# One attention-plus-MLP kernel: a pair's scores in two chained four-bank groups, its value product in one chain of column halves

## The chip, the cores and the metric

One NeuronCore of one Trainium2 chip. The metric is the device time of one launch, in microseconds. The kernel before took 706.77 us (median of 3 runs, 705.06 to 712.73).

## The reference

Three blocks follow one another, all in float32: an attention with a causal mask and a running-sum bias, a gated MLP that mixes over tokens, and a second mixing block with sines and cosines. Batch is 4, heads 8, sequence S = 576, head size D = 64, model width 512.

```
scores = q @ k.T / sqrt(D)
cum    = cumsum(max(s, 0))                       # over the sequence, per head
scores = where(causal, -1e9, scores + min(cum[key] - cum[query], 0))
attn   = softmax(scores);  x = attn @ v
h = gelu(x @ w_in); u, v = halves of h; v = layernorm(v) * g
x = x + (u * (w_sg @ v + b_sg)) @ w_out
theta = x @ w_theta; y = w_tok_r @ (x cos theta) + w_tok_i @ (x sin theta)
u = x + y;  out = u + max(u @ w_ch, 0)
```

## The kernel before

**Order of the stages.** The running sums of all 32 heads are made first (`cumulate`, L175), written to memory (L842) and read back, per pair of heads, spread over all 128 partitions (`load_cum`, L248). Then come 16 pairs of heads (4 per batch) of attention; the first MLP of batch b (`ffn`, L531) is used as filler on TensorE while batch b+1 runs its attention. After the last pair come the MLP of the last batch, its output product, and the second mixing block, which the change does not touch.

**A pair of heads** has three parts, which run one pair apart from each other (`attention`, L431): scores of pair p, transposes of the exponentials of pair p-1, value product of pair p-2. The string `ORDER` (or `ORDER_V`, where a value product takes part) gives the order by hand: `s` a score unit, `t` a transpose unit (one PSUM bank of up to four 128x128 transposes), `v` a piece of the value product, `r` the read of the reciprocals, `p` the preparation of later pairs (running sums, the splitting of Q and K into high and low parts, loads of Q, K and v). The framework then orders the instructions of each engine by these priorities and by a simulated clock of its own: an instruction whose inputs are not ready there is overtaken by a later one that is. On the chip each engine's order is fixed.

**Score units** (L285 to L318). The 576 queries are cut in five tiles, the last one into two key halves: six units of 64, 192, 320, 448, 288 and 288 key columns. A unit takes two PSUM banks, one for each head. Contraction is over 64 numbers, so the two heads use the two 64-row halves of TensorE, at the same time where their matmuls follow one another. There are three products for each unit (high-high, low-high, high-low) and up to two mask products of 128 columns in bfloat16. `row` (L100) forces the order within a unit, but lets other matmuls in between. VectorE evicts each unit and head with one instruction that adds the running sum and takes the row minimum (L307); ScalarE makes the exponentials and their sums (L313).

**PSUM.** Three buffers of two banks (`psS`, L235) serve score units, the value product and, from pair 4 on, the transposes; two single banks (`psF`) serve the MLP, and the transposes of pairs 0 to 3.

**Value product** (`pv_units`, L380). The first 64 keys of both heads are one full-width product (`v0` against `E0`: 512 columns, and 64 columns for the remaining queries); the other keys are products of 64 output columns each, one for each head, on the two column halves of TensorE. It is issued in three pieces, with other work between. These are float32 matmuls, which appear as two records each.

**Filler.** Each unit yields a cost in ns; `pace` (L110) adds it times a ratio (0.94 in `ffn_in`, 0.66 in `ffn_gate`) to a credit and issues that much of the MLP's matmuls, at a priority ten steps later. There is no filler before pair 4's end, since the MLP of batch 0 needs all four of its pairs. The conversion of the float64 weight w_in (`convert_in`, L500) is queued behind the load of pair 5's Q.

Of the kernel before, what the change touches and what calls it, by code (L numbers as in the profile page):

```python
# [32 lines left out]
UNITS = [(0, 0, 64), (1, 0, 192), (2, 0, 320), (3, 0, 448), (4, 0, 288), (4, 288, 288)]  # L33
# [19 lines left out]
class Kernel:  # L53
# [7 lines left out]
    ORDER = "sststtrspttststt"  # L61
    ORDER_V = "svststtrvspttsvtstt"
# [37 lines left out]
    def row(self, calls):  # L100

        before = None
        for c in calls:
            with ExitStack() as es:
                if before is not None:
                    es.enter_context(self.tc.issue_after(before.ins))
                before = self.mm(*c)
# [67 lines left out]
    def cumulate(self, es):  # L175
# [58 lines left out]
    def attention_psum(self, es):  # L234
        self.psS = self.pool(es, "psS", bufs=3, side="right", space=PSUM)  # L235
# [39 lines left out]
    def score_units(self, pr):  # L275
# [9 lines left out]
        for t, a, n in UNITS:  # L285
            w = max(n, P)
            qs = slice(QS[t], QS[t] + P)
            o = self.psS.tile([P, 2, 512], F32, name="sc", tag="sc")
            masks = (0, 1) if a + n == QE[t] else ()
            if t == 0:  # L290
                masks = (0,)
            calls = []
            for i, (x, y) in enumerate(((qh, kh), (ql, kh), (qh, kl))):
                for j, js in enumerate(halves):
                    calls.append((o[:, j, 0:w], x[js, qs], y[js, a:a + w], i == 0, i == 2 and not masks))
            for m in masks:
                for j, js in enumerate(halves):
                    calls.append((o[:, j, w - P:w], self.mlow[js, m], self.mpick[js, 64 - 64 * m:192 - 64 * m],
                                  False, m == masks[-1]))
            self.row(calls)  # L300

            c = (t - 1) % 5
            first, last = a == 0, a + n == QE[t]
            for j in (0, 1):
                at = E[:, EOFF[t] + a:EOFF[t] + a + n, j]
                d = c if last else 5
                nc.vector.tensor_tensor_reduce(  # L307
                    at, o[:, j, 0:n], C[:, j, a:a + n], -1.0, BIG if first else negm[:, j, 5:6],
                    ALU.add, ALU.min, negm[:, j, d:d + 1])
            if last:  # L310
                for j in (0, 1):
                    at = E[:, EOFF[t]:EOFF[t] + QE[t], j]
                    nc.scalar.activation(at, at, AF.Exp, bias=negm[:, j, c:c + 1], scale=-1.0,  # L313
                                         accum_out=sm[:, j * 5 + c:j * 5 + c + 1])
            if (t, a) == UNITS[-1][:2]:
                nc.vector.tensor_scalar(sm, sm, 1e-9, None, op0=ALU.add)
                nc.vector.reciprocal(r[:, 0:10], sm)
            yield 3 * max(107.0, w / 2.4) + 120 * len(masks) + 120  # L318

    def transpose_units(self, pr):  # L320
# [7 lines left out]
        T2 = None  # L328
# [51 lines left out]
    def pv_units(self, pr):  # L380
# [5 lines left out]
        YZ = self.psS.tile([P, 2, 512], F32, name="Y", tag="sc")  # L386
        Y, Z = YZ[:, 0], YZ[:, 1, 0:64]

        def pair(kt, a, c, n, stop):
            for i, F in enumerate(Efs):  # L390
                js = slice(i * D, i * D + D)
                self.mm(Y[js, a:a + n], vr[:, kt - 1, js], F[:, c:c + n], False, stop)
# [13 lines left out]
        yield 1700.0  # L406
# [420 lines left out]
    def run(self):  # L827
        nc = self.nc
        with ExitStack() as root, ExitStack() as right2, ExitStack() as left2:
# [157 lines left out]
```

## Time and profile before

| | |
|---|---|
| median of 3 runs | 706.77 us |
| profiled execution | 712.19 us |
| its span | 710.5 us |
| TensorE busy | 668.9 us (94%) |
| VectorE busy | 442.5 us (62%) |
| ScalarE busy | 367.1 us (52%) |
| GpSimd busy | 185.1 us (26%) |

The span is the time from the first to the last instruction of the program; the 1.7 us between it and the execution's time lie around it. Busy time of TensorE contains the modelled tail of each matmul: a matmul of 288 columns shows 0.29 us, while the next one starts 0.13 us after it. What one costs in a dense stretch is read from the distance between starts, not from the duration shown. Two rows that start a few ns apart and have half the rows or columns of the array each run side by side.

### The profile page before, as it was taken

The page shows a single profiled execution, that of the slowest core. Times are in us where ns is not written, and L with a number is a line of the kernel's source. Part 1 is how long each engine was busy: PE and PEld are TensorE (multiplying, and loading weights), DVE is VectorE, ACT ScalarE, POOL GpSimd, SP SyncE. Part 2 cuts the span into 40 slices and gives each one's busy share as a digit, 9 for nine tenths or more (in the row PEclk, how much of TensorE's full clock was granted, in tenths as well). Part 3 has the DMA queues.
Part 4 walks back from the last instruction along what each step waited for, and adds up shares of the span by engine and source line. Part 5 has one row for each costly group of instructions (what it writes and reads, how often), then busy time and mean ns, then how long its engine had stood idle before and what let it go on. Part 6 is the DMA issues. An engine that isn't in the chain of part 4 may idle for free.

```text
span 710.5 us, 12556 instructions
## 1 busy us (share of the span) xinstructions
PE 668.9 (94%) x4604; PEld 561.0 (79%) x4604; DVE 442.5 (62%) x1109; ACT 367.1 (52%) x840; POOL 185.1 (26%) x211
## 2 busy tenths in 40 slices
PE   4997889999999999999999779899999999999998
PEld 3654447877777777777779679788999989989997
DVE  4657784745546554564458898898876368367522
ACT  2757656774368743676427544584744256156100
POOL 4213351433223333232247662424000100010000
PEclk9999899999999999999999989999999999999999
DMA  6537662124321343210143689973000300300101
GB/s 181 162 105 244 215 192 84 52 101 150 123 96 68 101 136 133 78 57 19 52 152 110 222 254 300 299 255 117 33 1 29 106 1 1 134 1 0 69 1 66
DMA packets 46829, 79.95 MB, mean 113 GB/s; under 512 B 8048, under 2 KB 17680, under 8 KB 46768
## 3 DMA queue, kind: packets, MB, share of 16 engines
q1 hardware_dynamic: 46768, 79.16, 33.8%
q8 instruction: 36, 0.59, 0.3%
q14 instruction: 25, 0.20, 0.1%
HBM read 60.11 MB, written 19.03 MB: 111 GB/s over the span
## 4 chain that ended last, share of the span: by engine, by line
PE 76%; DVE 8%; DMA 7%; ACT 5%; issue 2%; POOL 1%; SPq 0%; DVEq 0%; ACTq 0%; POOLq 0%
PE fo L98 17%; PE yo L98 16%; PE sc L98 8%; PE Y L98 8%; PE th L98 7%; PE co L98 7%; PE T L342 6%; PE wo L98 5%; DMA wraw<-in_moe_w_in 2%; DMA x2T<-x2d 1%; DVE wta L477 1%; PE tp L730 1%; ACT uT L656 1%; DVE wta L476 1%; DMA gr<-gd 1%
## 5 line engine op out<-in xcount | busy, mean ns | idle before, releaser
L313 ACT ACTIVATE E<-E,negm 128x64 f32<-128x64 f32 (+4 forms) x160 | 93.1, 586 | 40.1 <-DVE negm L307 38.9
L307 DVE CUSTOM_DVE_ANT_0 E<-sc,C 128x64 f32<-128x64 f32 (+4 forms) x160 | 62.0, 427 | 53.2 <-PE sc L98 49.0
L98 PE MATMUL yo<-wkh,zh 128*128 128x288 f32 x288 | 85.2, 296 | 0.2 <-DVE x2T L803 0.2
L98 PE MATMUL yo<-wkl,zh 128*128 128x288 f32 x288 | 84.9, 296 | 0.0
L98 PE MATMUL yo<-wkh,zl 128*128 128x288 f32 x288 | 84.8, 296 | 0.0
L342 PE MATMUL T<-ident,E 128*128 128x128 f32 x400 | 73.0, 307 | 6.0 <-ACT E L313 2.7
L342 PEld LDWEIGHTS T<-ident,E 128*128 128x128 f32 x400 | 55.8, 195 | 16.0 <-ACT E L313 3.5
L98 PE MATMUL fo<-x,wih 128*128 128x288 f32 x256 | 55.8, 303 | 0.0
L98 PEld LDWEIGHTS yo<-wkh,zh 128*128 128x128 f32 x288 | 54.1, 188 | 0.7 <-DVE x2T L803 0.4
L98 PEld LDWEIGHTS yo<-wkl,zh 128*128 128x128 f32 x288 | 54.0, 188 | 0.3
L98 PEld LDWEIGHTS yo<-wkh,zl 128*128 128x128 f32 x288 | 53.9, 188 | 0.1
L98 PE MATMUL co<-u,wch 128*128 128x288 f32 x256 | 53.0, 295 | 0.0
L98 PEld LDWEIGHTS sc<-kh,qh 64*128 64x128 f32 x192 | 21.1, 203 | 38.6 <-issue 25.6
L98 PE MATMUL sc<-kh,qh 64*128 64x128 f32 (+2 forms) x192 | 42.7, 418 | 8.2 <-DVE negm L307 7.0
L98 PE MATMUL wo<-gh,woh 128*128 128x288 f32 x128 | 39.8, 314 | 9.1 <-DVE xr L707 6.4
L98 PE MATMUL fo<-wih,x 128*128 128x512 f32 x128 | 44.1, 407 | 3.0 <-ACT x L87 1.2
L91 POOL TENSOR_SCALAR xt<-x2s 128x128 fp32r<-128x128 f32 x16 | 11.0, 705 | 136.0 <-DVE x2s L95 136.0
L98 PE MATMUL Y<-Ef,vr 128*64 128x384 f32 (+3 forms) x256 | 46.4, 457 | 0.0
L98 PEld LDWEIGHTS fo<-x,wih 128*128 128x128 f32 x256 | 41.7, 188 | 3.5 <-issue 1.6
L98 PE MATMUL th<-wth,x2s 128*128 128x512 f32 x128 | 43.8, 409 | 0.0
L98 PEld LDWEIGHTS co<-u,wch 128*128 128x128 f32 x256 | 41.7, 188 | 0.0
L95 POOL TENSOR_TENSOR x<-xT,x 128x576 fp32r<-128x576 f32 x16 | 23.8, 1489 | 64.1 <-ACT x L87 64.1
(176 smaller groups left out, 1797.7 us busy)
## 6 DMA issues: line engine op xcount, KB each, us to landing
C<-cd SPq DMA_DIRECT2D x16, 576.0 KB, 4.3
Q<-in_q SPq DMA_DIRECT2D x16, 288.0 KB, 3.2
K<-in_k SPq DMA_DIRECT2D x16, 288.0 KB, 3.7
xT<-rd SPq DMA_DIRECT2D x32, 144.0 KB, 2.9
xd<-xT SPq DMA_DIRECT2D x16, 288.0 KB, 2.7
gd<-uT SPq DMA_DIRECT2D x16, 288.0 KB, 2.4
gr<-gd SPq DMA_DIRECT2D x16, 288.0 KB, 3.7
xr<-xd SPq DMA_DIRECT2D x16, 288.0 KB, 3.5
```

The lines of the kernel that those rows point to most:

```text
L91: nc.gpsimd.tensor_scalar(out, src, 1.0, 1.0, op0=ALU.mult, op1=ALU.mult)
L95: e.tensor_tensor(out, a, f32(hi), op=ALU.subtract)
L98: return self.nc.tensor.matmul(out, lhsT, rhs, start=start, stop=stop)
L307: nc.vector.tensor_tensor_reduce(at, o[:, j, 0:n], C[:, j, a:a + n], -1.0, BIG if first else negm[:, j, 5:6], ALU.add, ALU.min, negm[:, j, ...
L313: nc.scalar.activation(at, at, AF.Exp, bias=negm[:, j, c:c + 1], scale=-1.0, accum_out=sm[:, j * 5 + c:j * 5 + c + 1])
L342: nc.tensor.transpose(T[:, col:col + P], e, self.ident)
L476: nc.vector.tensor_scalar(ta.bitcast(U32), ta.bitcast(U32), 3, None, op0=ALU.logical_shift_left)
L477: nc.vector.scalar_tensor_tensor(ta.bitcast(U32), Hi, 0x80000000, ta.bitcast(U32), op0=ALU.bitwise_and, op1=ALU.bitwise_or)
L656: nc.scalar.activation(uT, uT, AF.Gelu_apprx_tanh)
L730: nc.tensor.transpose(tp[0:r, dt * P:(dt + 1) * P], x2T[:, dt, a:a + r], self.ident)
```

## The change

Five things change.

1. The six score units are put in two groups (`GROUPS`), each with all its matmuls in one chain, on one buffer of four PSUM banks. In the first group two units share a bank: 64 and 320 columns, 192 and 288 columns. The second group has the units of 448 and 288 columns. The products come low parts first.
2. `row` now gives each matmul of a chain but the first a high priority, so that nothing comes between.
3. The value product is one chain. The first 64 keys, too, are taken as two column halves, and the 64-column product comes last. It has two banks, one each for `Y` and `Z`, of a new pool `psT` of two single banks; this pool also serves the transposes (from pair 4 on all of them, before that every other bank).
4. `ORDER` and `ORDER_V` are written anew, with two `s` and one `v`.
5. At the start, each half of the running sums is written to memory and read back for pair 0 as soon as it is evicted; this part has high priority; pair 0 is split, and pair 1 loaded, before the v of pair 0.

```diff
-UNITS = [(0, 0, 64), (1, 0, 192), (2, 0, 320), (3, 0, 448), (4, 0, 288), (4, 288, 288)]
+GROUPS = [[[(0, 0, 64, 0), (2, 0, 320, 128)], [(1, 0, 192, 0), (4, 0, 288, 192)]],
+          [[(3, 0, 448, 0)], [(4, 288, 288, 0)]]]
...
-    ORDER = "sststtrspttststt"
-    ORDER_V = "svststtrvspttsvtstt"
+    ORDER = "sttsptrtttt"
+    ORDER_V = "sttsptrvtttt"
...
     def row(self, calls):
...
                 if before is not None:
+                    es.enter_context(self.tc.high_priority())
                     es.enter_context(self.tc.issue_after(before.ins))
                 before = self.mm(*c)
...
             nc.vector.tensor_copy(cpos[:, a:a + n], o[0:32, 0:n])
+            nc.sync.dma_start(self.cd[:, a:a + n], cpos[:, a:a + n])
+            self.load_cum(0, a, n)
...
-        self.psS = self.pool(es, "psS", bufs=3, side="right", space=PSUM)
+        self.psS = self.pool(es, "psS", side="right", space=PSUM)
+        self.psT = self.pool(es, "psT", bufs=2, side="right", space=PSUM)
...
-    def load_cum(self, pr):
-        C = self.a1.tile([P, 2, S], F32, name="C", tag="C", bufs=2)
-        self.nc.sync.dma_start(C, self.cd[2 * pr:2 * pr + 2].unsqueeze(0).to_broadcast([P, 2, S]))
-        self.cums[pr] = C
+    def load_cum(self, pr, a=0, n=S):
+        if a == 0:
+            self.cums[pr] = self.a1.tile([P, 2, S], F32, name="C", tag="C", bufs=2)
+        self.nc.sync.dma_start(self.cums[pr][:, :, a:a + n],
+                               self.cd[2 * pr:2 * pr + 2, a:a + n].unsqueeze(0).to_broadcast([P, 2, n]))
...
-        for t, a, n in UNITS:
-            w = max(n, P)
-            qs = slice(QS[t], QS[t] + P)
-            o = self.psS.tile([P, 2, 512], F32, name="sc", tag="sc")
...
-            for i, (x, y) in enumerate(((qh, kh), (ql, kh), (qh, kl))):
...
+        for group in GROUPS:
+            calls, sums, cost = [], [], 0.0
+            four = self.psS.tile([P, 4, 512], F32, name="sc", tag="sc")
+            for i, bank in enumerate(group):
+                o = four[:, 2 * i:2 * i + 2]
+                for t, a, n, col in bank:
+                    w = max(n, P)
...
+                    for k, (x, y) in enumerate(((qh, kl), (ql, kh), (qh, kh))):
+                        for j, js in enumerate(halves):
+                            calls.append((o[:, j, col:col + w], x[js, qs], y[js, a:a + w],
+                                          k == 0, k == 2 and not masks))
...
+                    sums.append((o, t, a, n, col))
+                    cost += 3 * max(107.0, w / 2.4) + 120 * len(masks) + 120
             self.row(calls)
+            for o, t, a, n, col in sums:
...
+                    nc.vector.tensor_tensor_reduce(
+                        at, o[:, j, col:col + n], C[:, j, a:a + n], -1.0, BIG if first else negm[:, j, 5:6],
+                        ALU.add, ALU.min, negm[:, j, d:d + 1])
...
+            yield cost
...
         def bank(i):
-            nonlocal T2
-            if early:
+            if early and i:
                 return self.psF.tile([P, 512], F32, name="T", tag="fo")
-            if i == 0:
-                T2 = self.psS.tile([P, 2, 512], F32, name="T", tag="sc")
-            return T2[:, i]
+            return self.psT.tile([P, 512], F32, name="T", tag="T")
...
-        YZ = self.psS.tile([P, 2, 512], F32, name="Y", tag="sc")
-        Y, Z = YZ[:, 0], YZ[:, 1, 0:64]
...
-        self.mm(Y, v0, E0[:, 0:512], True, False)
-        yield 950.0
-        pair(1, 0, 0, 512, False)
-        yield 950.0
-        self.mm(Z, v0, E0[:, 512:576], True, True)
-        for kt, a, c, n in ((2, 128, 512, 384), (4, 384, 896, 128), (3, 256, 1024, 256)):
-            pair(kt, a, c, n, kt == 3)
+        Y = self.psT.tile([P, 512], F32, name="Y", tag="T")
+        Z = self.psT.tile([P, 512], F32, name="Z", tag="T")[:, 0:64]
+        calls = []
+        halves = [slice(i * D, i * D + D) for i in (0, 1)]
+        for js in halves:
+            calls.append((Y[js], v0[:, js], E0[:, 0:512], True, False))
+        for kt, a, c, n in ((1, 0, 0, 512), (2, 128, 512, 384), (4, 384, 896, 128), (3, 256, 1024, 256)):
+            for js, F in zip(halves, Efs):
+                calls.append((Y[js, a:a + n], vr[:, kt - 1, js], F[:, c:c + n], False, kt == 3))
+        for js in halves:
+            calls.append((Z[js], v0[:, js], E0[:, 512:576], True, True))
+        self.row(calls)
...
-        yield 1700.0
+        yield 3600.0
...
-            self.cumulate(cs)
-            nc.sync.dma_start(self.cd, self.cpos)
-            self.load_cum(0)
+            with self.tc.high_priority():
+                self.cumulate(cs)
+            self.split_pair(0)
+            self.load_pair(1)
             self.load_v(0)
-            self.load_pair(1)
-            self.split_pair(0)
```

## Rows read from the trace of the kernel before

**Rows 1.** The page, busy time and share of the span.

```profile
PE 668.9 (94%) x4604; PEld 561.0 (79%) x4604; DVE 442.5 (62%) x1109; ACT 367.1 (52%) x840; POOL 185.1 (26%) x211
```

**Rows 2.** Windows: length; busy us of PE, PEld, DVE, ACT, POOL; granted clock; DMA.

```profile
16.00:52.00 36.00, 34.78 (x214) 23.02 (x214) 20.86 (x84) 22.91 (x73) 6.50 (x6) 1.00 0.44 135
52.00:101.00 49.00, 37.42 (x221) 20.23 (x221) 39.63 (x99) 31.81 (x86) 21.20 (x18) 0.90 0.72 230
101.00:366.00 265.00, 263.29 (x1932) 203.68 (x1931) 141.08 (x437) 156.21 (x386) 79.77 (x88) 1.00 0.27 91
```

**Rows 3.** TensorE's timeline around the last score unit of pair 10 (start, us).

```profile
229.51 0.29 PE L98 MATMUL fo<-x,wih 128*128 128x288 f32 x1
229.73 0.40 PE L98 MATMUL sc<-kh,qh 64*128 64x288 f32 x2
229.97 0.29 PE L98 MATMUL sc<-kh,ql 64*128 64x288 f32 x2
230.10 0.29 PE L98 MATMUL sc<-kl,qh 64*128 64x288 f32 x2
230.24 0.28 PE L98 MATMUL sc<-mpick,mlow 64*128 64x128 bf16 x4
230.45 0.40 PE L98 MATMUL fo<-x,wih 128*128 128x288 f32 x1
230.69 0.29 PE L98 MATMUL fo<-x,wil 128*128 128x288 f32 x1
230.82 0.43 PE L98 MATMUL fo<-x,wih 128*128 128x288 f32 x2
```

**Rows 4.** The same view, where two score units of pair 9 adjoin.

```profile
194.00 0.23 PE L98 MATMUL sc<-mpick,mlow 64*128 64x128 bf16 x2
194.04 0.34 PE L98 MATMUL sc<-kh,qh 64*128 64x192 f32 x2
194.22 0.27 PE L98 MATMUL sc<-kh,ql 64*128 64x192 f32 x2
194.33 0.27 PE L98 MATMUL sc<-kl,qh 64*128 64x192 f32 x2
```

**Rows 5.** The same view, where transposes cut a score unit of pair 10.

```profile
208.85 0.32 PE L98 MATMUL sc<-kh,qh 64*128 64x128 f32 x1
209.10 0.66 PE L342 MATMUL T<-ident,E 128*128 128x128 f32 x4
```

**Rows 6.** The same view, the value product of pair 8.

```profile
213.09 1.02 PE L98 MATMUL Y<-E,v 128*128 128x512 f32 x2
214.03 0.36 PE L98 MATMUL sc<-kh,qh 64*128 64x192 f32 x2
215.34 1.08 PE L98 MATMUL Y<-Ef,vr 128*64 128x512 f32 x4
216.35 0.43 PE L98 MATMUL Y<-E,v 128*128 128x64 f32 x2
216.72 1.52 PE L98 MATMUL Y<-Ef,vr 128*64 128x384 f32 x12
218.16 0.40 PE L98 MATMUL fo<-x,wih 128*128 128x288 f32 x1
```

**Rows 7.** The page, the eviction of the score units (busy, mean ns; idle before).

```profile
L307 DVE CUSTOM_DVE_ANT_0 E<-sc,C 128x64 f32<-128x64 f32 (+4 forms) x160 | 62.0, 427 | 53.2 <-PE sc L98 49.0
```

**Rows 8.** The chain of waits, early part: start, us, what.

```profile
8.48 2.99 DMA cd<-cpos
11.53 3.98 DMA C<-cd
52.75 0.42 SPq L243
53.22 5.94 DMA wraw<-in_moe_w_in
```

**Rows 9.** TensorE's timeline, a score unit of pair 0.

```profile
18.03 0.47 PE L98 MATMUL sc<-kh,ql 64*128 64x288 f32 x2
18.27 0.47 PE L98 MATMUL sc<-kl,qh 64*128 64x288 f32 x2
```

More of the change, by code (lines that the diff above doesn't have):

```diff
@@ L283, in score_units @@
         halves = [slice(j * D, j * D + D) for j in (0, 1)]
-        for t, a, n in UNITS:
-            w = max(n, P)
-            qs = slice(QS[t], QS[t] + P)
-            o = self.psS.tile([P, 2, 512], F32, name="sc", tag="sc")
[L289 to L292, printed above, removed]
-            for i, (x, y) in enumerate(((qh, kh), (ql, kh), (qh, kl))):
[L294 to L299, printed above, removed]
-            self.row(calls)
[L302 to L310, printed above, removed]
-                for j in (0, 1):
[L312 to L315, printed above, removed]
@@ new lines, in score_units @@
+        for group in GROUPS:
[5 more added lines that the diff above has]
+                    w = max(n, P)
+                    qs = slice(QS[t], QS[t] + P)
+                    masks = (0, 1) if a + n == QE[t] else ()
+                    if t == 0:
+                        masks = (0,)
+                    for k, (x, y) in enumerate(((qh, kl), (ql, kh), (qh, kh))):
+                        for j, js in enumerate(halves):
+                            calls.append((o[:, j, col:col + w], x[js, qs], y[js, a:a + w],
+                                          k == 0, k == 2 and not masks))
+                    for m in masks:
+                        for j, js in enumerate(halves):
+                            calls.append((o[:, j, col + w - P:col + w], self.mlow[js, m],
+                                          self.mpick[js, 64 - 64 * m:192 - 64 * m], False, m == masks[-1]))
+                    sums.append((o, t, a, n, col))
+                    cost += 3 * max(107.0, w / 2.4) + 120 * len(masks) + 120
+            self.row(calls)
+            for o, t, a, n, col in sums:
+                c = (t - 1) % 5
+                first, last = a == 0, a + n == QE[t]
+                for j in (0, 1):
+                    at = E[:, EOFF[t] + a:EOFF[t] + a + n, j]
+                    d = c if last else 5
+                    nc.vector.tensor_tensor_reduce(
+                        at, o[:, j, col:col + n], C[:, j, a:a + n], -1.0, BIG if first else negm[:, j, 5:6],
+                        ALU.add, ALU.min, negm[:, j, d:d + 1])
+                if last:
+                    for j in (0, 1):
+                        at = E[:, EOFF[t]:EOFF[t] + QE[t], j]
+                        nc.scalar.activation(at, at, AF.Exp, bias=negm[:, j, c:c + 1], scale=-1.0,
+                                             accum_out=sm[:, j * 5 + c:j * 5 + c + 1])
+            if group is GROUPS[-1]:
@@ L316, in score_units @@
                 nc.vector.tensor_scalar(sm, sm, 1e-9, None, op0=ALU.add)
                 nc.vector.reciprocal(r[:, 0:10], sm)
-            yield 3 * max(107.0, w / 2.4) + 120 * len(masks) + 120
+            yield cost
     def transpose_units(self, pr):
@@ L327, in transpose_units @@
         early = pr < H // 2
-        T2 = None
         def bank(i):
-            nonlocal T2
-            if early:
+            if early and i:
                 return self.psF.tile([P, 512], F32, name="T", tag="fo")
-            if i == 0:
-                T2 = self.psS.tile([P, 2, 512], F32, name="T", tag="sc")
-            return T2[:, i]
+            return self.psT.tile([P, 512], F32, name="T", tag="T")
         def transposed(T, j, blocks):
@@ L385, in pv_units @@
         xT = self.xTs.pop(pr)
-        YZ = self.psS.tile([P, 2, 512], F32, name="Y", tag="sc")
-        Y, Z = YZ[:, 0], YZ[:, 1, 0:64]
[L389 to L392, printed above, removed]
-        self.mm(Y, v0, E0[:, 0:512], True, False)
-        yield 950.0
-        pair(1, 0, 0, 512, False)
-        yield 950.0
-        self.mm(Z, v0, E0[:, 512:576], True, True)
-        for kt, a, c, n in ((2, 128, 512, 384), (4, 384, 896, 128), (3, 256, 1024, 256)):
-            pair(kt, a, c, n, kt == 3)
+        Y = self.psT.tile([P, 512], F32, name="Y", tag="T")
[10 more added lines that the diff above has]
+        self.row(calls)
         nc.vector.tensor_tensor(xT[:, 512:576], Z, xT[:, 512:576], op=ALU.mult)
```

## The prediction, made before the changed kernel was run

> **What bounds the kernel now.** I read busy shares first, then stretches, then single matmuls. The page gives TensorE 94% of the span and no other engine over 62% [rows 1]. The windows divide the part that the change touches in three [rows 2]. From 101 to 366 us TensorE has 263.3 of 265 us, VectorE and ScalarE little over half: whatever shortens TensorE's stream there shortens the kernel by as much. From 52 to 101 us TensorE has 37.4 of 49, VectorE 39.6, and the DMA share is 0.72: this is the stretch in which w_in is converted, and it hangs on loads and on VectorE. From 16 to 52 us TensorE again has nearly all. After 366 us nothing changes but the moment at which it starts.
>
> In the full stretch the useful part of TensorE's time is smaller than it looks. Take the distances between starts [rows 3]. Two MLP matmuls in a row are 0.13 us apart (230.69, 230.82). The last one before a score unit holds 0.22 (+0.09). The unit's first product takes 0.24, its second 0.13 (+0.11). The four mask rows, side by side in twos, take 0.21, where 256 columns at 2.4 GHz are 0.11 (+0.10). The first MLP matmul behind takes 0.24 (+0.11). So one stay in half-array matmuls costs **0.41 us beyond its columns**, whatever its length: TensorE changes shape on the way in and on the way out. Where two units adjoin, the join costs 0.18 against 0.11 for the unit's first product, less 0.01 at the mask: 0.06 [rows 4].
>
> **The change, part by part.**
>
> *Scores.* Pairs 9 to 12 have 24 units; one join [rows 4] makes it one stay less, two units cut in two by transposes (one is shown [rows 5]; the other is pair 12's) make two more: 25 stays. Two unbroken groups a pair leave 8 stays and 16 joins. 17 stays x 0.41 = 7.0 us, less 15 new joins x 0.06 = 0.9: 6.1 us in four pairs, 1.5 a pair. Scores of 11 pairs lie in the full stretch: 16.7 us. The columns, the mask products and VectorE's and ScalarE's instructions stay the same in number and size; the order of the three products costs nothing, since the low part of K is made a pair ahead.
>
> *Value product.* Now, start to next start [rows 6]: 0.94 (first keys, full width), 1.01, 0.37 (64 columns, full width), 1.44, together 3.76 us. The 1.01 of both heads' 512 columns contains the change of shape; the columns alone, two passes of 512 at two cycles, are 0.85 at 2.4 GHz. In the chain that stands twice, 0.85 each; the 1.44 for the other keys stays; the 64 columns take 0.11. That is 3.25: 0.51 less, of which 0.09 was the way into a score unit and is counted above: 0.42 x 13 products = 5.5 us. That halves of 64 columns really run side by side is seen in the four records of 512 columns, which take 1.01 together and not twice 0.85.
>
> *Hand-overs.* New is that one four-bank buffer serves all scores. Group 2 waits until the eight evictions of group 1 are done, the next pair's group 1 for four more. Evictions take 62.0/16 = 3.9 us a pair [rows 7], by columns 2.1 in group 1 and 1.8 in group 2. Group 1's chain is about 1.8 us (928 columns x 3 at 0.13 per 288, five mask steps of 0.05, one first step, three joins); its first pair of banks is complete 0.9 us before the end, so VectorE, at 2.1 us for the eight, needs another 1.2 us behind it, more with other work in front. Between the groups stand two transpose units (four transposes show 0.66 with their tail [rows 5], so about 1 us for eight) and filler for the cost that the group and the two units yield (0.94 x 3.4 = 3.2 us), 4 us in all. The wait is covered while there is filler. I take 0.3 us a pair for what is badly timed, 3 us; the ends are 0 and 3.0 a pair (both hand-overs bare: 1.5 each).
> The trace of this kernel has no unit that shares a bank with another, so what that does to the first eviction is bounded: it starts between 0 and 0.6 us later (the 320 columns of its neighbour, three products of 0.15), within the 4 us of cover. The Trainium skill, "PSUM — Partial Sum Buffer", section "Summary: rules for kernel authors", asks that PSUM be read in another bank than the one that a matmul writes; by that it is 0.6 here, and the sum is the same.
>
> *New order.* Preparation of a pair (`p`) stands after its second group, with six DMA issues as before, on SP; the scores of pair p+1 come later than they did, so nothing waits there. In the chain of the value product both banks of `psT` are taken, and the next transposes wait for it and for two VectorE instructions on 576 columns (0.8 us at the 0.43 per 320 of [rows 7]); filler of 3.4 us (0.94 x 3.6) stands there. I cost this at nothing; without filler it is 0.8 us a pair. The longer row of exponentials on ScalarE (59% busy in the full stretch [rows 2]) can hold an MLP bank for a while; that is in the 0.3.
>
> *Start.* The first eviction waits for memory: write at 8.48, 2.99 us, read at 11.53, 3.98 us [rows 8]. The first half is ready about 1.5 us sooner. Its write and read are two more DMA issues, and the second half's may queue behind them on SP, where the read waits for the write: it can then land 1.5 us later than now. Between -1.5 and +1.5 I take 0.5 us saved.
>
> *The stretch from 16 to 101 us.* Here the price is open. Until some 40 us TensorE ran at its lower level: 288 columns take 0.24 us [rows 9] against 0.13 later [rows 3], 1.2 against 2.4 GHz, although the window prints 1.00. Stays cost more there, and two and a half pairs of scores lie in it; pair 2's matmuls must end before pair 4 can be split, and only behind that, at 52.75, goes the load of pair 5's Q, with the first w_in load right after it [rows 8]. Denser chains bring this forward: 2 to 4 us a pair over three pairs, 6 to 12 us. From there on the conversion and VectorE's 39.6 of 49 us decide, and may hand all of it back. Ends 0 and 12; I take **6 us**, the middle, since VectorE's rows bear out neither end.
>
> *Sum.* 16.7 + 5.5 - 3 + 0.5 + 6 = 25.7 us. From the profiled 712.19 that is 686.5; this execution is 5.4 us over the median of 706.77, so against the median **681 us**.
>
> **The rivals.**
>
> *A. The early stretch gives all, and no wait is left:* 16.7 + 5.5 + 1.5 + 12 = 36 us, 671 us. For it: TensorE idles 11.6 us from 52 to 101 [rows 2]. Against: w_in's loads come one after another on SP, behind attention's waits.
>
> *B. Part is handed back:* VectorE and ScalarE get their work in bursts, MLP banks stay full for longer, and waits take 1 us a pair (11 us), while the early stretch gives nothing or TensorE stays at 1.2 GHz there for longer. 22.2 - 11 - 2 = 9 us, 698 us (690 to 705). For it: two MLP banks only; between VectorE's bursts the first four pairs have no filler. A clock that stays low is part of it: the products of a pair (1664 columns, three times) are 2.3 us at 0.13 per 288 columns and 4.2 at the 0.24 of [rows 9], 2 us a pair. The granted clock is 0.90 in the stretch in which TensorE idles [rows 2]. The Trainium skill, "TensorE: Matmul & The Clock Gate", section "Why this matters for your kernels", warns of idle gaps between bursts of matmuls for that reason; the trace agrees.
>
> *C. Slower: the hand-overs lie bare.* If the fixed order of TensorE puts the second group before VectorE is done, both hand-overs cost 1.5 us, and a Q split or an MLP eviction in front of them another 1 (put so, no row prices it): 4 us a pair, against 1.9 gained. Over 16 pairs 64 - 30 = 34, of which I leave half, since filler still covers some: 706.8 + 17 = 724 us. It decides from 1.9 us a pair on. Against it: the 4 us of cover, and that now, with TensorE full for 265 us, it idles for under 2.
>
> *D. The chains do not hold:* MLP matmuls still come between, and the stays remain. 705 us.
>
> **How the numbers follow.** Forecast 0.50, A 0.20, B 0.18, C 0.08, D 0.04. The range of 8 in 10, 664 to 702, holds the forecast (673 to 690 with its open terms), A with the doubt in its early term, and most of B. A measurement of this kernel tells 1% (about 7 us) from no change: faster means under 699.7, slower over 713.8. Forecast, A and two thirds of B are faster: 0.82; the rest of B and D are the same: 0.10; C is slower: 0.08.
>
> **What would show it.** In TensorE's timeline in the middle of the full stretch: each pair's groups unbroken runs of 34 and 20 score records, 8 stays in four pairs, the value product 24 records in one run of some 3.3 us. The full stretch is 246 us long in place of 265 (16.7 + 5.5 - 3 less). Little idle time of TensorE behind VectorE's minima; if that wait is over 1 us a pair, C or B is on its way. The chain of waits should show the first w_in load at 41 to 47 us, and the full stretch should begin at 95 or sooner. What follows the last pair should be as long as now. The prediction is wrong if the stretch before the full one grows, or if the stays get fewer and the pairs no shorter.

## The result and the profile after

The changed kernel takes 688.56 us (median of 4 runs, 688.21 to 689.13), the kernel before 706.60 in the same comparison (4 runs, 705.06 to 712.73): a ratio of 0.973, 95% interval 0.9672 to 0.9787, so 18.0 us faster where 25.7 were forecast. 688.6 lies inside the range of 664 to 702. The profiled executions are 23.1 us apart: 689.13 us (span 687.1) against 712.19 (710.5).

The page of the changed kernel, busy time and share of the span; beside [rows 1], TensorE has lost 30.6 us of busy time and the other engines little:

```profile
PE 638.3 (93%) x4668; PEld 556.6 (81%) x4668; DVE 436.5 (64%) x1109; ACT 362.7 (53%) x838; POOL 186.0 (27%) x211
```

The windows that answer to [rows 2], with the same columns (length; busy us of PE, PEld, DVE, ACT, POOL; granted clock; DMA share, GB/s). Attention now ends at 342 us in place of 366:

```profile
16.00:52.00 36.00, 31.36 (x271) 22.74 (x273) 25.72 (x100) 26.67 (x87) 8.42 (x8) 0.88 0.58 187
52.00:101.00 49.00, 36.90 (x266) 26.79 (x261) 42.20 (x106) 32.53 (x86) 21.27 (x18) 0.79 0.63 205
101.00:342.00 241.00, 236.35 (x1889) 192.99 (x1889) 126.75 (x409) 148.17 (x366) 78.20 (x86) 1.00 0.31 97
```

The full stretch is full as it was. In the 49 us before it TensorE executes 266 matmuls in place of 221. The granted clock is 0.79 there, 0.90 before; but a second profile of the kernel before (e1) has 0.83, so that this is no more than executions of one kernel differ by.

TensorE's timeline in the full stretch (start, us, engine, line, tiles, form, count), in three places: group 1 of pair 8 and the start of its group 2; the value product of pair 6, cut before its last product; that of pair 7, which is not cut. It answers to [rows 3, 4, 6]:

```profile
145.52 0.33 PE L99 MATMUL sc<-kl,qh 64*128 64x128 f32 x2
145.69 0.28 PE L99 MATMUL sc<-kh,ql 64*128 64x128 f32 x2
145.80 0.27 PE L99 MATMUL sc<-kh,qh 64*128 64x128 f32 x2
145.91 0.23 PE L99 MATMUL sc<-mpick,mlow 64*128 64x128 bf16 x2
...
147.42 0.29 PE L99 MATMUL sc<-kh,qh 64*128 64x288 f32 x2
147.64 0.40 PE L99 MATMUL fo<-wsh,vh 128*128 128x288 f32 x1
...
153.05 0.29 PE L99 MATMUL fo<-wsrl,vh 128*128 128x288 f32 x1
153.28 0.47 PE L99 MATMUL sc<-kl,qh 64*128 64x448 f32 x2
...
155.34 1.08 PE L99 MATMUL Y<-E,v 128*64 128x512 f32 x4
156.25 2.32 PE L99 MATMUL Y<-Ef,vr 128*64 128x512 f32 x16
158.51 0.40 PE L99 MATMUL fo<-wsh,vh 128*128 128x288 f32 x1
158.75 0.29 PE L99 MATMUL fo<-wsl,vh 128*128 128x288 f32 x1
...
159.15 0.29 PE L99 MATMUL fo<-wsh,vh 128*128 128x288 f32 x1
159.37 0.34 PE L99 MATMUL Z<-E,v 128*64 128x64 f32 x4
159.63 0.40 PE L99 MATMUL fo<-wsl,vh 128*128 128x288 f32 x1
...
170.39 1.08 PE L99 MATMUL Y<-E,v 128*64 128x512 f32 x4
171.30 2.32 PE L99 MATMUL Y<-Ef,vr 128*64 128x512 f32 x16
173.45 0.28 PE L99 MATMUL Z<-E,v 128*64 128x64 f32 x4
173.66 0.40 PE L99 MATMUL fo<-wsrh,vh 128*128 128x288 f32 x1
```

Group 1 is one run of 34 records, 2.12 us from its first start to the MLP matmul behind it (145.52 to 147.64), and group 2 one of 20 in 1.51 us. The price of a stay stands as before: 0.24 for the first MLP matmul behind (147.64, or 158.51 to 158.75) in place of 0.13. What the prediction did not have is at 158.51: in 7 of the 12 value products of the full stretch the 64-column product `Z` comes 0.9 to 1.5 us late, with MLP matmuls in between. In six of them it makes a second stay; in the seventh it stands against a score group.

Not every matmul with half of the columns pays. The half-width MLP product (`fo<-wil,x`, 64 columns of the array) stands between full ones here, and the next start comes 0.23 us behind it (111.01 to 111.24), as it does behind the full ones (0.22 and 0.24):

```profile
110.79 0.39 PE L99 MATMUL fo<-wih,xt 128*128 128x512 f32 x1
111.01 0.39 PE L99 MATMUL fo<-wil,x 128*64 128x512 f32 x1
111.24 0.40 PE L99 MATMUL fo<-wih,xt 128*128 128x512 f32 x1
111.48 0.39 PE L99 MATMUL fo<-wil,x 128*64 128x512 f32 x1
```

Why this product is exempt is not shown.

VectorE's timeline, behind group 1 of that pair: the evictions of the group begin at 149.47, 1.8 us after its last product, because the eviction of a transpose bank (`E<-T`) stands in front of them in VectorE's order. They are done at 151.96, and group 2 begins at 153.28. The wait of [rows 7] is covered all the same, since 5.6 us of other matmuls stand between the groups.

```profile
148.86 0.69 DVE L380 COPY E<-T 128x512 f32<-128x512 f32 x1 [2.54 <-PE T L351]
149.47 0.21 DVE L320 CUSTOM_DVE_ANT_0 E<-sc,C 128x64 f32<-128x64 f32 x1
...
151.51 0.45 DVE L320 CUSTOM_DVE_ANT_0 E<-sc,C 128x288 f32<-128x288 f32 x1
```

What TensorE waited for (us in total, times, longest us), first from 7 to 101 us, then from 101 to the end of attention:

```profile
PE T L351 <- ACT E L326: 11.4, 5, 6.5
PE sc L99 <- DVE negm L320: 4.7, 1, 4.7
...
PE fo L99 <- ACT uT L653: 1.9, 7, 0.6
...
PE T L351 <- DVE Ef L363: 0.7, 1, 0.7
PE T L351 <- DVE xT L408: 0.6, 1, 0.6
PE sc L99 <- DVE negm L320: 0.5, 2, 0.3
```

In the early stretch the transposes' wait for exponentials has grown (11.4 us, 2.7 before); scores waited for VectorE there before, too (4.7 us now, 7.0 before). In the full stretch scores wait 0.5 us in all.

The chain of waits, early part (start, us, what), beside [rows 8]. The first read of the running sums is issued at 11.31 (VectorE's first eviction is at 13.6, was 15.7); the first w_in load at 47.89, 5.3 us sooner than before (53.22), where 6 to 12 were forecast:

```profile
11.31 0.37 SPq L257
...
47.89 0.42 SPq L478
48.37 5.91 DMA wraw<-in_moe_w_in
```

**An account of TensorE from 101 us to the last value product.** For each kernel the distances from start to next start in TensorE's timeline, less idle time, are summed by the tile written (records, us). A *stay* is an unbroken run of score and value-product records that use half of the array's rows or columns; the half-width MLP products aren't counted. The last row is the time in this stretch at the lower of TensorE's two clocks (granted clock 0.50, 1.2 GHz).

| | before | after | pieces (e2) | no priority (e3) | both (e11) | two banks (e4) | two buffers (e10) |
|---|---|---|---|---|---|---|---|
| length | 264.9 | 241.5 | 248.9 | 252.0 | 253.2 | 243.4 | 252.7 |
| scores | 594, 47.2 | 532, 35.9 | 540, 37.2 | 540, 41.5 | 540, 40.9 | 506, 38.3 | 522, 37.4 |
| value product | 45.8 | 40.4 | 42.6 | 41.4 | 45.9 | 40.9 | 40.6 |
| transposes | 312, 39.1 | 301, 35.4 | 303, 35.4 | 300, 37.6 | 301, 36.2 | 293, 33.4 | 301, 35.4 |
| MLP | 784, 131.0 | 769, 125.2 | 769, 126.0 | 769, 127.4 | 769, 128.0 | 761, 126.5 | 769, 129.6 |
| idle | 1.7 | 4.7 | 7.7 | 4.0 | 2.2 | 4.1 | 9.2 |
| stays | 91 | 37 | 37 | 63 | 70 | 48 | 41 |
| at half the clock | 0 | 0 | 6.8 | 1.7 | 3.4 | 6.8 | 13.1 |

### The profile page after: what moved, and what is told of

It is laid out like the page before. It is cut to its first block, busy times and chain, and to the rows that moved or that the text cites. A ratio compares the mean times of both kernels' runs of the same rounds, so it can differ in the third digit from the quotient of the medians.

```text
span 687.1 us, 12585 instructions
## 1 busy us (share of the span) xinstructions
PE 638.3 (93%) x4668; PEld 556.6 (81%) x4668; DVE 436.5 (64%) x1109; ACT 362.7 (53%) x838; POOL 186.0 (27%) x211
## 4 chain that ended last, share of the span: by engine, by line
PE 64%; DVE 10%; DMA 10%; ACT 9%; POOL 4%; issue 2%; SPq 1%; DVEq 0%; ACTq 0%; POOLq 0%
PE yo L99 17%; PE fo L99 15%; PE co L99 7%; PE th L99 6%; PE sc L99 5%; PE T L351 5%; PE Y L99 5%; ACT E L326 3%; PE wo L99 3%; POOL vT L583 2%; DMA wraw<-in_moe_w_in 2%; DMA K<-in_k 2%; DMA x2T<-x2d 1%; DVE E L320 1%; ACT vT L633 1%
## 5 line engine op out<-in xcount | busy, mean ns | idle before, releaser
L326 ACT ACTIVATE E<-E,negm 128x64 f32<-128x64 f32 (+4 forms) x160 | 92.8, 586 | 12.3 <-DVE negm L320 12.1
L351 PE MATMUL T<-ident,E 128*128 128x128 f32 x400 | 64.8, 293 | 18.5 <-ACT E L326 11.4
L351 PEld LDWEIGHTS T<-ident,E 128*128 128x128 f32 x400 | 54.3, 193 | 25.6 <-ACT E L326 13.3
L320 DVE CUSTOM_DVE_ANT_0 E<-sc,C 128x64 f32<-128x64 f32 (+4 forms) x160 | 58.8, 427 | 17.7 <-PE sc L99 14.2
L99 PE MATMUL fo<-x,wih 128*128 128x288 f32 x256 | 57.3, 305 | 1.9 <-ACT uT L653 1.9
L363 DVE COPY Ef<-T 128x512 f32<-128x512 f32 x32 | 22.0, 689 | 39.8 <-PE T L351 35.9
L99 PE MATMUL sc<-kl,qh 64*128 64x128 f32 (+2 forms) x192 | 39.4, 404 | 5.8 <-DVE negm L320 5.2
L88 ACT CAST u<-x2T 128x576 fp32r<-128x576 f32 x16 | 10.7, 670 | 58.2 <-DVE x2T L809 58.1
L686 POOL TENSOR_TENSOR uT<-gt,uT 128x288 f32<-128x288 f32 x32 | 27.3, 854 | 48.5 <-DVE gt L684 40.7
```

The source lines that it names most:

```text
L88: nc.scalar.copy(out, src)
L99: return self.nc.tensor.matmul(out, lhsT, rhs, start=start, stop=stop)
L320: nc.vector.tensor_tensor_reduce(at, o[:, j, col:col + n], C[:, j, a:a + n], -1.0, BIG if first else negm[:, j, 5:6], ALU.add, ALU.min, ne ...
L351: nc.tensor.transpose(T[:, col:col + P], e, self.ident)
L363: nc.vector.tensor_copy(Ef[:, 512:1024], T)
L686: nc.gpsimd.tensor_tensor(uT[:, ft, a:a + m], gt, uT[:, ft, a:a + m], op=ALU.mult)
```

## The experiments

Times are medians; the ratio is to the kernel before, run beside it. That kernel's own median was 706.60 in the comparison above and 708.95, 709.98, 710.36 and 709.89 in the four below, so kernels of different comparisons are set side by side by ratio; the changed kernel's is 0.973.

**e1, the kernel before once more.**

> The kernel before, profiled once more. Its four timed runs are 705 to 707 with one of 712.7, and the profiled one was 712.2. If the 5 us lie in the stretch before 101 us (loads of w_in, VectorE's queue), a profile of 706 us will show the full stretch starting 5 us sooner, at about 96, with the same 265 us behind it; if they lie behind the attention, the full stretch starts at 101 again and the tail of 344.6 us is shorter.

707.82 us. Its last value product ends at 364.4 us and 341.7 us follow; in the profile that the prediction was made from it was 365.9 and 344.6. So 4.4 of that execution's 5.4 us above the median belong to the one execution and not to the program: 1.5 us before the end of attention and 2.9 behind it. Neither of the two places expected was the place alone. The granted clock of the early stretch differs by execution as well; e1's windows, with the columns as above:

```profile
16.00:52.00 36.00, 33.06 (x220) 21.39 (x218) 22.06 (x85) 24.19 (x75) 8.16 (x8) 0.77 0.47 150
52.00:101.00 49.00, 38.48 (x236) 21.55 (x236) 39.09 (x100) 30.60 (x82) 18.41 (x16) 0.83 0.68 220
```

**e2, the value product in its three pieces again.**

```diff
-    ORDER_V = "sttsptrvtttt"
+    ORDER_V = "sttsptrvvvtttt"
...
-        self.row(calls)
+        self.mm(Y, v0, E0[:, 0:512], True, False)
+        yield 950.0
+        pair(1, 0, 0, 512, False)
+        yield 950.0
+        self.mm(Z, v0, E0[:, 512:576], True, True)
...
```

> The changed kernel with the value product as before: first keys at full width, three pieces, the 64-column product in the middle, no chain (all three pieces at the place of the one). Theory (changes of the array's shape cost the time): 0.42 us a pair in 13 pairs, 5.5 us slower than the changed kernel, 694. Rival (the gain came from the new order and the filler, not from the chain): 688 to 689 as the changed kernel.

695.00 us, ratio 0.9818 (0.9787 to 0.9849): 6.4 us slower than the changed kernel by medians, 0.9% (6.2 us) by ratio. In the account only 2.2 us are in the value product's own rows, since the three pieces, put one behind the other, mostly ran together (37 stays as in the changed kernel). 3.0 us are idle time; the rest is in score and MLP rows, 6.8 us of this stretch having run at half the clock. The forecast came true, but as a price of the value product alone it can't be read.

**e3, the chains without their priority.**

```diff
                 if before is not None:
-                    es.enter_context(self.tc.high_priority())
                     es.enter_context(self.tc.issue_after(before.ins))
```

> The changed kernel without the high priority in row: the order within a chain stays forced, but other matmuls may come between. Theory: each break of a chain costs one more stay, 0.35 us; with one break in each of the 48 chains 17 us, 705; if the simulated clock lets few in, say one in three, 6 us, 694. Rival (the groups are what counts, nothing gets in between anyway): 688 to 689 and the same number of runs of score records.

694.19 us, ratio 0.9789 (0.976 to 0.9819); attention ends 10.5 us later. TensorE's timeline shows what comes back: an MLP matmul amid a unit, 0.33 us long (148.28 to 148.61), and the next product takes 0.26, a unit's price of entry again. Against an unbroken chain (0.15 for each product of 320 columns, 0.13 for the MLP matmul) that is 0.08 + 0.20 + 0.11 = 0.39.

```profile
148.05 0.30 PE L99 MATMUL sc<-kh,ql 64*128 64x320 f32 x2
148.28 0.40 PE L99 MATMUL fo<-wsh,vh 128*128 128x288 f32 x1
148.61 0.41 PE L99 MATMUL sc<-kh,qh 64*128 64x320 f32 x2
148.87 0.23 PE L99 MATMUL sc<-mpick,mlow 64*128 64x128 bf16 x2
```

In the account e3 has 26 more stays in the full stretch (63 against 37), and it is 10.5 us longer. Of this 0.9 us are lost to 1.7 us at the lower clock and 0.5 are eight more score records, while 0.7 less is idle: 9.8 us for 26 stays, **0.38 us a stay**, against 0.41 in the prediction. This is the main theory's price, with the groups, buffers and order strings unchanged. It rests on one profile of each kernel. The profiled execution is the slowest of the four (697.18), and what follows attention is 2.9 us shorter in it; whole times differ by 5.6 us by medians and by 0.6% (4.2 us) by ratio, where the two intervals overlap.

**e4, four groups of two banks, two buffers.**

```diff
+GROUPS = [[[(0, 0, 64, 0), (2, 0, 320, 128)]], [[(1, 0, 192, 0), (4, 0, 288, 192)]],
+          [[(3, 0, 448, 0)]], [[(4, 288, 288, 0)]]]
...
+    ORDER = "ssttssptrtttt"
+    ORDER_V = "ssttssptrvtttt"
...
+        self.psS = self.pool(es, "psS", bufs=2, side="right", space=PSUM)
...
```

> The changed kernel with four groups of one pair of banks on two buffers in place of two groups on one buffer of four banks; the first two and the last two follow one another in the order. Theory (hand-overs are covered, TensorE waits 0.5 us for VectorE's minima in the full stretch): nothing to gain there, 687 to 690, unless groups drift apart and make stays: up to 2 x 0.35 x 11 = 8 us slower. Rival (the single buffer holds the early pairs back, where no filler is): the full stretch starts 3 to 5 us sooner, 684.

688.06 us, ratio 0.9722 (0.9685 to 0.976): no difference to the changed kernel. It does more early, 325 matmuls from 52 to 101 us in place of 266, at a granted clock of 0.92 in place of 0.79; TensorE idles about as long from 16 to 101 us (15.6 us, 16.7 in the changed kernel). But behind 101 us there are 11 more stays, and `Z` of one value product waits 2.4 us for ScalarE, behind which 6.8 us run at half the clock; attention ends 1.9 us later. From 16 us on the waits for exponentials are nearly gone (from 7 us on they are 4.5 us in place of 11.4), and others, for ScalarE's copies of transposes, stand in their place. The last line is from 101 us on:

```profile
PE T L351 <- ACT Ef L359: 5.7, 2, 5.4
PE Y L99 <- ACT Ef L359: 3.1, 1, 3.1
...
PE T L351 <- ACT E L326: 1.1, 1, 1.1
...
PE Z L99 <- ACT rT L372: 2.4, 1, 2.4
```

**e5, the start as before.**

```diff
-            nc.sync.dma_start(self.cd[:, a:a + n], cpos[:, a:a + n])
-            self.load_cum(0, a, n)
...
+            nc.sync.dma_start(self.cd, self.cpos)
+            self.load_cum(0)
...
```

> The changed kernel with the start of the kernel before: running sums written and read in one part, no high priority there, v of pair 0 before pair 1's loads and pair 0's split. In the changed kernel the first eviction starts at 13.6 us (before 15.7), but the 320-column unit, which needs the second half, holds VectorE until 15.5 us, and group 2 follows at 17.8. Theory (the early stretch is set by the w_in conversion, not by the start): 688 to 690, nothing to be told from the changed kernel. Rival (the start's 2 us reach the end): 690.5.

689.38 us, ratio 0.9711 (0.9671 to 0.975): no difference. The first eviction is at 15.8 in place of 13.6, and nothing comes of it: in the changed kernel VectorE evicts 64 columns of both heads, then stands 1.5 us for the second half of the running sums.

**e6 and e7, the conversion of w_in moved.** e6 lets it follow earlier loads; e7 puts its second half behind the store of pair 3's result.

```diff
-    FROM = (10, 10, 11)
+    FROM = (8, 8, 9)
```

```diff
-    FROM = (10, 10, 11)
+    FROM = (10, "x3", 11)
...
+        if b == 0 and pr == 3:
+            self.loaded["x3"] = wr
```

> The changed kernel with the loads of w_in and w_sg queued behind the Q of pair 4, a pair sooner. Theory (in the changed kernel pair 3's value product ends at 87.6 us, but its eviction waits until 92.8, because VectorE and ScalarE, in order, stand at the conversion of w_in's second half, whose load lands at 87.2): loads 10 us sooner take that wait away, the full stretch starts 4 to 6 us sooner, 683 to 685. Rival (VectorE's sum of work bounds the stretch, it is 70.6 of 94 us busy from 7 to 101): the conversion only pushes pairs 2 and 3 back, 687 to 690.

> The changed kernel with the second half of w_in loaded only behind the store of pair 3's result, so that nothing of it stands before that eviction. Theory: the eviction comes at 88 instead of 92.8 us, the MLP's first half starts 5 us sooner, 683 to 685, unless the second half (needed some 20 us later) is then late: its four loads and conversions take some 16 us. Rival (VectorE's sum of work): no more than 1 us.

e6: 691.57 us, 0.9735 (0.9701 to 0.977), with the first w_in load at 36.7 us. e7: 690.35 us, 0.9724 (0.9691 to 0.9757). Eleven microseconds on the first load (e6) bring nothing: the time of that load, on which the prediction's early term hung, does not decide. Both theories missed at their first step: VectorE's eviction of pair 3's value product, at 92.8 in the changed kernel, was to come some 5 us sooner, and comes at 97.5 in e6 and at 91.8 in e7.

**e8, the conversion without its bits.** The three VectorE instructions that put w_in's bits together are left out.

```diff
+        if bits:
             nc.vector.tensor_scalar(ta.bitcast(U32), ta.bitcast(U32), 3, None, op0=ALU.logical_shift_left)
             ...
```

> The changed kernel without the three VectorE instructions that put together w_in's float32 bits from its float64 words (the loads, the ScalarE and GpSimd steps stay): 24 instructions, about 14 us of VectorE's time between 52 and 105 us, gone. Rival (VectorE's sum of work bounds the early stretch): up to 8 us faster, 680. Theory (the order of the queues and the landing of the loads, not the sum): 2 to 4 us faster, 685 to 687.

687.46 us, 0.9675 (0.9635 to 0.9716). From 52 to 101 us VectorE has 28.75 us of work in place of 42.20, the hundredth MLP matmul comes at 126.2 us in place of 129.7, and attention still ends at 343.9, no sooner than the 342.5 of the changed kernel: 5.4 us of idle time and 4.9 us at half the clock stand in the full stretch. By ratio e8 is 0.5% below the changed kernel and the intervals overlap, so a gain of the 2 to 4 us that were expected is neither shown nor excluded; the 8 us of the rival, that VectorE's sum bounds the early stretch, are not seen.

**e9, early pairs in four chains, later pairs in two, over two buffers of two banks; e10, two buffers alone.**

```diff
+        self.psS = self.pool(es, "psS", bufs=2, side="right", space=PSUM)
...
-            four = self.psS.tile([P, 4, 512], F32, name="sc", tag="sc")
             for i, bank in enumerate(group):
-                o = four[:, 2 * i:2 * i + 2]
+                o = self.psS.tile([P, 2, 512], F32, name="sc", tag="sc")
```

e9 has besides, for pairs 0 to 5, each bank pair as a group of its own and the order strings of e4.

> Scores of pairs 0 to 5 in four chains of two PSUM banks, two buffers of two banks; from pair 6 on the two long chains of the changed kernel (each now over two buffers). Theory, that the early stretch loses TensorE time because a pair's exponentials all come late behind one four-bank group (11.4 us of waiting of transposes for ScalarE's exponentials before 101 us, nearly gone with chains of two banks): that wait under 3 us, the last value product at 338 to 341 in place of 342.5, the median 683 to 687, against 688.6. Rival, that the early stretch is set by loads and by the conversion of w_in and not by TensorE's waits: the waits go, but the first MLP matmul of the main run stays at 95 us, and the median at 688 to 690.

> The changed kernel with its four-bank buffer replaced by two buffers of two banks; groups, chains and order as they are: only the moment at which banks come free moves. Theory that the hand-over of the one buffer is covered by other work: nothing, 687 to 690, and the wait of score matmuls for VectorE's minima falls from 5.2 us to 2 to 4, most of it at pair 0. Rival, that the hand-over still costs the 0.3 us a pair that was forecast (in places where another instruction was put in front of the score group): 684 to 686.

Both theories of both runs missed: e9 692.98 us, 0.9761 (0.9736 to 0.9785), e10 695.73 us, 0.9791 (0.9765 to 0.9817), both slower than the changed kernel by medians, while by ratio their intervals overlap with its own (0.9672 to 0.9787). e10 should have done nothing or helped; in its profile attention ends 11.2 us later. The two buffers let the framework order the work otherwise: `Z` of a value product now stands amid a score chain, and waits there, with the chain behind it, for ScalarE's copy `rT`, which frees a bank of `psT`. TensorE's timeline of e10:

```profile
125.47 0.33 PE L99 MATMUL Z<-E,v 128*64 128x64 f32 x2 [1.41 <-ACT rT L371]
125.72 0.41 PE L99 MATMUL sc<-kh,qh 64*128 64x320 f32 x1
...
130.61 0.44 PE L99 MATMUL fo<-x,wil 128*128 128x288 f32 x1
130.85 0.57 PE L99 MATMUL fo<-x,wih 128*128 128x288 f32 x2
131.26 0.29 PE L99 MATMUL fo<-x,wil 128*128 128x288 f32 x1
131.39 0.43 PE L99 MATMUL fo<-x,wih 128*128 128x288 f32 x2
```

From 130.61 to 130.85 one MLP matmul takes 0.24, from 131.26 to 131.39 it takes 0.13. The windows of e10 around it (length, TensorE busy, granted clock, DMA share, GB/s) show the clock:

```profile
124.00:127.80 3.80, 2.39 (x28) 0.99 0.14 27
127.80:131.20 3.40, 3.40 (x17) 0.50 0.92 257
131.20:134.60 3.40, 3.40 (x29) 1.00 0.43 155
```

The 1.41 us of waiting is followed by a stretch at 1.2 GHz in which TensorE is busy throughout. In e10 13.1 us behind 101 us ran at that level, in the changed kernel none: these 3.4 us, 3.4 us from 223.3 on (TensorE had waited 2.7 us for ScalarE's `uT` from 220.9 on), and 6.3 us at the very start, behind a wait of 2.0 us in the early stretch. At half rate that is 6.5 us; with 4.5 us more idle time it makes 11.0 of the 11.2 us by which attention ends later (353.7). This profile is of the slowest of e10's five executions. `Z` waits in the same way, 2.4 us each time, in e4 and e9.

**e11, the value product in pieces and no priority.**

> Value product in three pieces as before, and no priority within chains: both at once. If the two prices are separate they add: 688.6 + 6.4 + 5.6 = 700.6, between 698 and 703; what then still parts it from the kernel before (708) is two groups in place of six units, the PSUM pools and the new order. Rival, that part of the 6.4 us of the value product is its unbroken chain, which the missing priority breaks as well: 695 to 698.

700.75 us, ratio 0.985 (0.9819 to 0.9881). By ratio e2 and e3 cost 0.9% and 0.6% of the kernel before; together 1.2%, against 1.5% if they added: within the intervals they do, and 700.75 is what was forecast. The value product's rows are back at 45.9 us with 45.8 before, and 4.5 us over e3's, which has its chain. The 1.5% that e11 still is below the kernel before belongs to groups, PSUM pools, order strings and start together; but for the start (e5) no run brings one of these back alone.

**e12, two pools.** As e9, but at pair 6 the two-bank pool is closed and the four-bank pool opened:

```diff
+            if p == self.CHAIN_FROM:
+                self.scores.close()
+                self.psS = self.pool(self.scores, "psS4", side="right", space=PSUM)
```

> Scores of pairs 0 to 5 in four chains of two banks from a pool of two two-bank buffers; at pair 6 that pool is closed and the four-bank pool of the changed kernel takes its place, with its chains and order. Theory, that the chains of two banks gain in the early stretch and that the kernel with early chains of two banks lost it only to waits that two buffers bring in the full stretch (4.2 us for the MLP's first half, 2.4 us for the reciprocals, 2.0 us for the value product's eviction): those waits back under 5 us in all after 101 us with no low clock there, 20 runs of score records after 100 us, the last value product at 338 to 341, the median 683 to 687. Rival, that the waits in the full stretch come from the order in which the MLP's first matmuls meet the pairs, whatever the buffers: waits of 7 us or more stay, and the median is at 689 to 693.

686.32 us, ratio 0.9663 (0.9631 to 0.9696), the lowest ratio of all; its interval overlaps that of the changed kernel (0.9672 to 0.9787), so 0.7% better is likely and not shown. The full stretch is mended, as the theory said: no low clock, 19 runs of scores; the waits came to 6.3 us, not under 5. e9 and e12 differ in the score buffers from pair 6 on alone, and their intervals lie apart (0.9761 and 0.9663; attention ends at 347.8 and 342.8): with two long chains the one four-bank buffer, which the prediction had as a pure cost, is better here than two of two banks. The early stretch is fuller, by its window from 52 us (same columns as above; the second row is the full stretch):

```profile
52.00:101.00 49.00, 41.11 (x314) 27.11 (x313) 36.66 (x101) 34.68 (x99) 20.90 (x17) 0.88 0.60 190
101.00:342.00 241.00, 234.67 (x1854) 190.66 (x1854) 128.63 (x412) 148.47 (x365) 79.10 (x86) 1.00 0.30 98
```

TensorE executes 314 matmuls from 52 to 101 us in place of 266, at a granted clock of 0.88 in place of 0.79. But the last value product ends at 342.8, not at 338 to 341: the theory that the early waits for exponentials cost the end of attention fell a second time. They fell from 11.4 to 4.9 us in e9 and e12, but TensorE's idle time from 16 to 101 us stayed nearly the same (16.2 and 15.5 us, 16.7 in the changed kernel), for other waits took their place. What its profiled execution has less, 2.3 us, lies behind attention.

## Why the prediction was right, and where it was not

**The price of a stay: right.** 0.41 us forecast, 0.38 by e3's account, 0.39 by its rows. This kernel pays it in parts: 0.09 before the stay, 0.11 behind, 0.21 inside. The Trainium skill, "TensorEngine Tiling (Array Packing)", section "Key Properties", says that a change of tiling mode drains TensorE, and gives no price; the rows show such a loss at each change between full matmuls and score or value-product records.

**Scores: right in kind.** 34 and 20 records in unbroken runs, 8 stays in four pairs. A pair's score rows went from 4.29 us (47.2 / 594 x 54) to 3.65. Group 1's chain takes 2.12 us, not 1.8: a product of 128 columns takes 0.11 us in it (145.69, 145.80, 145.91), where the prediction's rate by columns gives 0.06, and the 2.12 hold the way out (0.09).

**The value product: the columns right, the one run wrong.** 3.82 us a product before, 3.37 after (the account, 12 products), 0.45 less where 0.51 were forecast. But "24 records in one run" holds in 5 of the 12 only. A `Z` put off to a stay of its own costs 0.10 in `Y` (3.16 us from 155.34 to 158.51, 3.06 from 170.39 to 173.45), 0.11 behind `Y`, 0.09 before `Z` and 0.05 inside (0.26 from 159.37 to 159.63 against 0.21 from 173.45 to 173.66): 0.35 x 6 = 2.1 us.

**Sum of the full stretch.** Behind 101 us the changed kernel is 23.4 us shorter, but it also has less to do there: 62 score records, 11 transposes and 15 MLP matmuls of 512 columns fewer, at 0.0675, 0.12 and 0.23 us together 8.9 us. The same work therefore takes 14.5 us less. The forecast had 11 pairs and 13 products; for the 10.4 pairs and 12 products that this stretch holds, its own prices give 15.8 + 5.0 - 3 = 17.8. Of the 3.3 that lack 2.1 are `Z`'s; the rest such counting doesn't resolve.

**Hand-overs: the size right, the place wrong.** 3 us were set aside for scores waiting for evictions. They wait 0.5; idle time grew by 3.0 all the same, mostly at ScalarE's and VectorE's evictions of MLP and transpose banks, of which the prediction spoke in one clause. Rival C's mechanism (evictions behind another instruction on VectorE) is there at 149.47, but 5.6 us of cover swallow it. And e9 against e12 shows that two buffers cost more than the one.

**The early stretch: forecast near by luck.** 6.5 us were forecast with the start, and 1.4 more for the pairs and the product that lie there; 8.9 us' worth of work now stands before 101 us (7.3 against e1's profile). But the signs set for it failed. The first w_in load came at 47.89 (41 to 47 said). TensorE's last wait before the full stretch ends at 93.5 us, before at 95.3: 1.8 us sooner in place of 6. The start gives nothing (e5), nor does the moment of the loads (e6, e7), and the 8 us that a rival gave to VectorE's sum are not seen (e8). Shorter waits for exponentials (e9, e12) did not shorten TensorE's idle time in sum, which from 16 to 101 us is 14.0 to 17.3 us in the changed kernel and in all of e2 to e12; so what less of it would give is not tested. What decides this stretch is open.

**From 25.7 to 18.** The end of attention moved by 23.4 us against the profile of before, by 21.8 against e1. What follows was as long as then (344.6 in both profiles), but over the fourteen profiles it varies from 340.7 to 346.0, and by 2.9 between two profiles of the kernel before. The term that was mis-sized is the last: "this execution is 5.4 us over the median", and the whole saving carried over to the median. e1 shows that most of this excess was one execution's own; the changed kernel's profile is only 0.6 us over its median. 23.1 - 5.4 + 0.6 = 18.3 is what the medians show (706.77 less 688.56, but for rounding).

**The rivals.** A would need early signs that are not there. B's clock did not come true as a change: from 16 to 101 us the granted clock is 0.83 here and 0.80 in e1; a fall in the full stretch is seen in some of the experiments and not here. C and D are out: in the full stretch no score group waits for long, and the chains of scores hold.

## What to carry to other kernels

Where score or value products of half array shape alternate with full matmuls on TensorE, count the stays, not the matmuls: here each one costs 0.35 to 0.41 us whatever its length, and it is saved by putting work of the same shape side by side, which a priority on the chain's members does. Read from the distances which matmuls pay: the half-width MLP product did not. Before trusting a rebuilt order, look in the timeline for the member that a scarce PSUM bank pushes out of its chain (`Z` here): it pays the change of shape again. And take the saving from a pair of profiles only after a second profile of the kernel before: an execution that lies above its median does not hand that excess on, and the granted clock of its early part can be its own as well.

## What the hardware showed that was not expected

A wait of 1.41 us in a stretch that is otherwise full was followed, from 127.8 to 131.2 us, by a granted clock of 0.50 with TensorE busy throughout (e10). From 110 us to the end of attention the fourteen profiles have six such falls (one each in e2, e4, e8 and e9, two in e10), each behind a wait of 1.41 to 2.36 us or, in one case, at the end of one of 2.70 us, all for ScalarE. Not every such wait did it: four of 1.53 to 1.65 us (e9, e10) and one of 2.71 us (e9, from 216.4 to 219.1) were followed by no fall. The Trainium skill, "TensorE: Matmul & The Clock Gate", section "HAM oscillation — how this bites in real kernels", tells of such falls behind waits for transfers; here it was a wait for another engine, each time.
